# Sliding-window attention beside a state-space convolution on one core: stages put in pieces into one written order, eight shared PSUM banks, paired channels in the table product

## The chip, the cores and the metric

The kernel runs on one core of a Trainium2 chip. The metric is device time in microseconds (us) of one execution; lower is better. The engines are TensorE (PE, with PEld for its weight loads), VectorE (DVE), ScalarE (ACT), GpSimd (POOL) and SyncE (SP). SP and POOL mainly issue DMAs here. Every engine works through its own instructions in order. Matrix products land in PSUM, which has eight banks of 128 x 512 f32.

## The reference

Two independent parts are computed and joined along the last axis. S = L = 2048, D = 640, all inputs are bf16.

```python
# A: attention of 32 heads of 20 channels over the 8 positions s, s-2, ..., s-14
qkv = (x @ wqkv) -> q, k, v
logits = einsum("bhsd,bhswd->bhsw", q, kg) * 20 ** -0.5     # masked where s - 2w < 0
o = einsum("bhsw,bhswd->bhsd", softmax(logits), vg)
a = o.reshape(B, S, D) @ wo

# B: a convolution of length 2048 in each of 640 channels
K[d, l] = real(sum_n C[d, n] * exp(dt[d] * A[d, n] * l) * dt[d] * B[d, n])   # n < 192, A, B, C complex
y = irfft(rfft(u, 4096) * rfft(K, 4096))[:2048] + u * Dskip
```

## The kernel before, in words

Part B works in five chunks c of 128 channels each (four groups g of 32 channels). For a chunk it does the following.

- **Tables** (`Tables`, L314): DVE builds `Xtab` (20 powers) and `Ytab` (33 powers) from generators by complex products (`cmul`, L297: two products and two sums). `xtab` (L355) takes eight calls of `cmul`, `ypos` (L332) three, `yneg` (L347) multiplies by magnitudes that ACT made in `ymag` (L340). The generators of chunk 0 are put in place directly, those of chunks 1 to 4 go out to `Gdram` and come back by `loadx` and `loady` (L325 to L330).
- **Table product** (`kgen_part`, L386): four quarters q of eight channel indices each; every channel of a group has its own small matmul, 20 rows by 33 columns (L398 and L403), into one PSUM bank. ACT copies the bank to `Kd` (L405), and four DMAs on the POOL queue shift a part of it by one row (L383).
- **spread** (L408) and **f1** (L430), **f2** (L441): the kernel table and u are transformed to spectra. u was put into the order of `Udram` at the start: POOL loads `us`, DVE rearranges it to `uc` (L806), POOL stores it; the stage `u{c}` then loads one piece `U` (L820).
- **product** (L464) of the two spectra on DVE, after two DMAs that swap halves (L461), then **ia** (L470), the first half of the inverse. `Z` goes to DRAM for chunks 0 to 2, and stays for 3 and 4.
- **last0e, last1q** (`inverse`, L888): the second half of the inverse, with `HB`, plus u * Dskip (`uD`, L886). ACT copies to `ysb` (two buffers), SP stores it with four DMAs per piece (L902).

Part A runs in four blocks of 512 positions: `proj` (L509, PE, ACT copies `st`, SP stores to DRAM), `fetch` and `fetch_v` (L532, L541: loads of the shifted windows), `logits` (L554: ten elementwise products `prod` on DVE, sums over a head's channels on PE, exponential on ACT without a maximum, sum by PE, logarithm and exponential for the reciprocal, one product `attn` on DVE), `av` (L582: ten products `p` on DVE, sums on PE), `out_proj` (L604). `prod` and `p` share three buffers.

PSUM is shared out by tags: `a` has two banks (projections, `av`, output projection), `l` two (logits), `b` four (all of part B).

The order of the work is written out by hand: `SEQ` gives for each engine the words `stage:count`, and `chain` (L692) ties that engine's instructions together in this order. Within a stage the order is that of the code. The queues of SP and POOL are in `SEQ` too, so a DMA that waits holds everything behind it.

Of the kernel before, what the change touches and what calls it, by code (L numbers as in the profile page):

```python
# [48 lines left out]
def sel_consts_np():  # L49
# [9 lines left out]
    def add(Wm):  # L59
        full = np.zeros((128, 32), np.float32)  # L60
        for g in range(4):
            full[32 * g:32 * g + 32, 8 * g:8 * g + 8] = Wm
# [65 lines left out]
def att_consts_np():  # L128
    gs = np.zeros((128, 5, 32)); hs = np.zeros((128, 32)); sm = np.zeros((128, 128))
# [14 lines left out]
spec:15 out0:3 logits1:2 u1:8 logits1:2 out0:2 u1:2 out0:2 u1:2 out0 u1:2 logits1:4 u1:2 out0:2 spread0:8 out0:2 spread0:8 logits1:2 spread0:20
logits1:2 out0 logits1:4 spread0:8 logits1:4 out0:2 spread0:4 out0:2 spread0:2 out0 spread0:2 logits1:4 spec0:32 logits1:4 spec0 out0:4 spec0:16
out0:3 spec0:16 out0:2 spec0:15 out0 spec0:48 inv0:57 kgen20:129 inv0:7 logits1:8 kgen21 kgen22 kgen23:33 u2:2 logits1:2 kgen23:32 u2:2 logits1:2
kgen23:64 u2:2 kgen22:32 u2:2 kgen22:32 u2:4 kgen22:64 u2:4 kgen21:128 spread1:36 av1:6 spread1:8 av1:5 spread1:2 av1:8 spread1:2 av1:9 spread1:2
av1:9 spread1:2 av1:27 spec1:49 av1:15 spec1:16 av1 spec1:63 inv1:64 kgen30 kgen31:33 kgen30:32 kgen31:96 kgen30:96 kgen32 kgen33 u3:2 kgen33:32 u3:2
kgen33:32 u3:2 kgen33:32 u3:4 kgen33:32 kgen32:32 u3:6 kgen32:32 spread2:16 kgen32:32 spread2:20 kgen32:32 av1:21 spread2:8 av1:5 spread2:2 av1:8
spread2:4 av1:2 spread2:2 av1:12 spec2:6 logits2:4 spec2:26 av1:8 spec2 av1:19 spec2:16 av1:5 logits2:4 spec2:31 out1:2 logits2:4 spec2 out1:2  # L150
spec2:16 out1 spec2:15 out1:2 spec2 out1:3 spec2:15 out1:20 inv2:32 out1:7 inv2:25 kgen40:33 inv2:5 logits2:4 inv2:2 out1:2 kgen40:96 logits2:4 out1
logits2:4 kgen41 kgen42 kgen43 u4:2 kgen43:64 u4:2 kgen43:32 u4:2 kgen43:32 logits2:6 u4:2 logits2:2 u4:2 logits2:4 kgen42:32 u4:4 logits2:4 kgen42:32
u4:2 spread3:8 logits2:2 kgen42:32 spread3:8 logits2:2 spread3:12 kgen42:32 spread3:8 kgen41:32 spread3:6 kgen41:32 spread3:2 kgen41:32 spread3:6
av2:15 spread3:2 av2:33 kgen41:32 spec3:32 av2:8 spec3 av2:8 spec3:95 av2:43 inv3:32 av2:21 inv3:25 spread4:16 inv3:4 spread4:12 inv3 spread4:8 inv3:2
av2:16 spread4:16 av2:16 spec4:32 logits3:4 out2:2 spec4 logits3:2 spec4:16 logits3:2 out2:2 spec4:16 logits3:4 spec4:15 out2 spec4 logits3:4 spec4:16
out2:2 spec4:15 logits3:4 spec4 out2:2 spec4:15 logits3:4 out2:20 inv4:32 out2 logits3:4 out2:5 inv4:25 last00:18 inv4:7 logits3:12 out2:5 last01
logits3:2 last01:8 logits3:2 last01 last02 last01:8 last02:17 last03 av3:32 last03:9 last04 last03:8 av3:17 last04:17 av3:37 last05 av3:39 last05:17
av3:35 last06:10 out3:10 last06:8 out3:10 last07 out3:10 last07:17 last10:34 last11:17 out3:10 last11:17 last12:34 last13:34
""",
    mybir.EngineType.Activation: """  # L160
prep:11 am0:2 prep am0:9 weights:2 gens0:13 weights gens0:4 weights gens0:4 k0 gens0 mag0:3 k0 mag0:3 k0 mag0:2 k0 mag0:3 k0 mag0:2 q0 mag0:3 am1:11
gens1:5 q0:3 gens1 q0 v0:3 gens1 v0:2 gens1:2 k1:2 gens1 k1 gens1 k1 gens1 k1 gens1 q1 gens1 q1 gens1 q1 gens1 q1 gens1 q1 v1 gens1:2 v1 gens1 v1
gens1 v1:2 k2:2 gens1:2 k2:2 mag1:5 k2 mag1:3 q2:2 mag1:8 q2 kgen00 q2:2 kgen03 kgen02 kgen01 v2:5 k3:5 q3:5 mag2:16 kgen13 v3:2 logits0:2 v3:2 kgen10
v3 logits0:2 kgen11 kgen12 av0:2 u0:8 av0:2 spec:4 av0:2 spec:4 out0 spec:4 out0 spec:4 out0 u1:7 spread0:4 u1 out0 spread0:8 out0:2 spec0:6 out0
spec0:10 mag3:14 inv0:4 mag3:2 inv0:3 out0 kgen20 inv0 logits1:2 u2:2 logits1:2 kgen23 u2:4 kgen22 u2:2 kgen21 spread1:12 av1:2 spec1:16 mag4:8 inv1:7
mag4 inv1 mag4:7 kgen31 kgen30 u3:5 kgen33 u3:3 spread2:4 kgen32 spread2:8 av1:2 spec2:6 av1 spec2:4 av1 spec2:4 out1 spec2:2 out1:5 inv2:4 out1
inv2:4 kgen40 out1 u4:3 kgen43 u4:4 logits2:2 u4 spread3:2 logits2 spread3 logits2 spread3 kgen42 spread3:8 kgen41 spec3:16 av2:2 inv3:4 av2:2 inv3:3
spread4:4 inv3 spread4:8 av2:2 spec4:10 out2 spec4:6 out2:3 inv4:2 out2 inv4:2 out2:2 inv4:3 last00:2 inv4 logits3:2 out2 last01 logits3:2 last01
last02:2 av3:2 last03:2 av3:2 last04:2 av3:2 out3 last05:2 out3:3 last06:2 last07:2 out3:4 last10:2 last11:2 last12:2 last13:2
""",  # L170
    mybir.EngineType.DVE: """
prep:11 gens0 prep gens0:2 prep:2 gens0:2 genm0 gens0:2 genm0 gens0:2 genm0 gens0:2 genm0 gens0:2 genm0 gens0:2 genm0 gens0:2 genm0 gens0:2 genm0
gens0:2 genm0 gens0 weights genm0 ypos0 genm0 weights:10 xtab0 weights xtab0 gens1 xtab0:2 gens1 xtab0:2 gens1 xtab0:2 gens1 xtab0:2 u xtab0:8 gens1
genm1 xtab0 genm1 xtab0 gens1 xtab0:2 genm1 xtab0:4 gens1 xtab0:4 gens1 xtab0:2 gens1 ypos0 genm1 gens1:2 ypos0 gens1 genm1 gens1 ypos0 gens1 genm1
gens1 ypos0 gens1 genm1 gens1 ypos0 genm1 gens1:2 ypos0 gens1 genm1 gens1 ypos0 genm1 yneg0 gens1 yneg0 ypos0:2 genm1 ypos0:2 u yneg0:2 xtab1:22 u
xtab1:4 logits0 xtab1:4 logits0 xtab1:2 logits0 ypos1:2 logits0 ypos1:2 logits0 ypos1:2 logits0 ypos1:4 yneg1 ypos1:2 yneg1:2 u xtab2:2 yneg1 xtab2:2
logits0 xtab2:2 logits0 xtab2:2 logits0 xtab2:2 logits0 xtab2:8 logits0 xtab2 av0:8 xtab2 av0:2 xtab2 ypos2 xtab2 logits1 xtab2:4 logits1 xtab2:4
logits1 xtab2:2 logits1 ypos2 logits1 ypos2:2 logits1 ypos2:2 logits1 ypos2:2 logits1 ypos2 xtab3 ypos2 yneg2 ypos2:2 yneg2 xtab3 yneg2 prod0 xtab3
prod0:2 xtab3 prod0 xtab3:2 yneg2 xtab3:2 logits1 xtab3:2 logits1 xtab3:10 logits1 xtab3:2 av1 xtab3:4 av1 xtab3:4 av1 xtab3:2 ypos3:4 av1 ypos3:2
xtab4 ypos3:2 av1 ypos3:2 yneg3 ypos3:2 yneg3 xtab4 prod1 xtab4 prod1:2 xtab4 prod1 xtab4:2 yneg3 xtab4:2 yneg3 xtab4:2 av1 xtab4:2 av1 xtab4:2 av1  # L180
xtab4:18 av1:2 ypos4:2 logits2 ypos4:4 logits2 ypos4:2 logits2 yneg4 ypos4 yneg4 ypos4 prod2 ypos4 prod2:2 ypos4 prod2 yneg4 logits2 yneg4 logits2:7
av2:7 prod3:3 av2 prod3 av2 ud1 ud4 ud0 ud2 ud3 av2 logits3:6 prod4:3 logits3 prod4 logits3:4 av3:10
""",
# [432 lines left out]
def kernel(  # L618
# [213 lines left out]
    with at("fetch0"):  # L832
        a.fetch(0)
# [114 lines left out]
```

## Time and profile before

| | |
|---|---|
| median of three runs | 418.0 us |
| the three runs | 409.86, 418.0, 427.05 us |
| span of the profiled execution | 415.1 us (from the first to the last instruction; the page gives no other time of it) |
| PE busy | 316.8 us, 5645 matmuls |
| DVE busy | 307.1 us, 445 instructions |
| ACT busy | 262.1 us, 570 instructions |
| DMA | 70.67 MB in 78841 packets, 170 GB/s |
| table product on PE (L398 and L403) | 29.7 and 27.4 us, 1280 matmuls each |
| projections on PE (L515) | 76.4 us |
| `prod` and `p` on DVE (L562 and L592) | 48.2 and 47.4 us |
| `Xtab`, largest groups on DVE (L306 and L307) | 24.5 and 24.4 us |

How to read the profile: a line of a group gives engine, operation, output and inputs, shapes, count, busy time and the mean time of one. A line of waits gives who waited for whom, then the total in us, the number of times and the longest. "issue" is time in which an engine waited for nothing that the profile shows. In the timeline the first number is the start in us, the second the length, and the bracket is the idle time ahead of the group with what ended it. A window gives what moved in one stretch of the span.

### The profile page before, as it was taken

What the parts mean: (1) busy time and instruction counts of PE and PEld (TensorE: products, weight loads), DVE (VectorE), ACT (ScalarE), POOL (GpSimd) and SP (SyncE); (2) the same over time, 40 slices, a digit from 0 to 9 for tenths busy, and PEclk for the clock granted to TensorE, in tenths of its full rate; (3) what the DMA queues carried; (4) which work ended last, traced back from release to release, by engine and by line L of the source; (5) the groups of instructions that cost most, each with busy time, mean ns of one, the idle gap of its engine ahead of it and who ended that gap; (6) DMA issues with size and microseconds to landing.
All of it is one profiled execution on the core that took longest, in us unless ns stands there. A gap on an engine that the chain in (4) does not pass through costs nothing. (4 is left out here: it accounts for less than half of the span.)

```text
span 415.1 us, 13105 instructions
## 1 busy us (share of the span) xinstructions
PE 316.8 (76%) x5645; PEld 196.1 (47%) x5654; DVE 307.1 (74%) x445; ACT 262.1 (63%) x570; POOL 50.4 (12%) x101
## 2 busy tenths in 40 slices
PE   0569249989359988799788886799999875897781
PEld 0224114335233355356476556565666663475561
DVE  0558978995974999589999599959972765786500
ACT  0587977987004533489976596469747977573552
POOL 7453300004014010200000200011000400000000
PEclk9999959999759999589979696779999988799996
DMA  5999765668998847869308530727166499616656
GB/s 75 217 212 178 202 164 190 214 216 260 207 213 205 271 126 171 233 146 254 114 17 230 154 86 2 205 64 154 51 195 209 138 369 313 137 49 177 160 134 95
DMA packets 78841, 70.67 MB, mean 170 GB/s; under 512 B 35264, under 2 KB 73904, under 8 KB 76992
## 3 DMA queue, kind: packets, MB, share of 16 engines
q1 hardware_dynamic: 71616, 54.96, 51.3%
q0 software_dynamic: 4144, 12.18, 11.9%
q10 hardware_dynamic: 3024, 2.70, 2.9%
q8 instruction: 44, 0.72, 0.7%
q14 instruction: 13, 0.11, 0.1%
HBM read 37.82 MB, written 23.65 MB: 148 GB/s over the span
## 5 line engine op out<-in xcount | busy, mean ns | idle before, releaser
L515 PE MATMUL ps_p<-xT,w 128*128 128x512 bf16 x291 | 76.4, 409 | 20.9 <-ACT st L516 15.4
L515 PEld LDWEIGHTS <-w 128*128 128x128 bf16 x300 | 30.0, 103 | 60.3 <-issue 33.3
L562 DVE TENSOR_TENSOR prod<-qk 128x2048 bf16<-128x2048 bf16 x40 | 48.2, 1225 | 11.6 <-PE ps_l L566 8.9
L592 DVE TENSOR_TENSOR p<-vb,attn 128x2048 bf16<-128x2048 bf16 x40 | 47.4, 1224 | 12.1 <-PE ps_o L598 12.0
L438 ACT CAST A<-ps_f 128x512 bf16<-128x512 f32 x80 | 42.8, 613 | 19.0 <-PE ps_f L437 18.6
L516 ACT CAST st<-ps_p 128x512 bf16<-128x512 f32 x60 | 34.6, 586 | 23.1 <-PE ps_p L515 21.1
L456 ACT CAST Sp<-ps_f 128x512 bf16<-128x512 f32 (+1 forms) x96 | 42.4, 564 | 4.6 <-PE ps_f L452 3.5
L398 PE MATMUL ps_k<-Ytab,Xtab 128*20 128x33 bf16 x1280 | 29.7, 248 | 15.1 <-issue 15.1
L598 PE MATMUL ps_o<-p,cHs 64*32 64x256 bf16 x640 | 27.7, 297 | 12.5 <-DVE p L592 7.7
L452 PE MATMUL ps_f<-A,cT 64*128 64x128 bf16 (+1 forms) x768 | 29.4, 211 | 5.4 <-ACT Sp L456 3.5
L398 PEld LDWEIGHTS <-Xtab 128*20 128x20 bf16 x1280 | 23.3, 128 | 21.6 <-issue 20.2
L405 ACT CAST Kd<-ps_k 128x264 bf16<-128x264 f32 x20 | 7.6, 380 | 40.7 <-PE ps_k L403 40.5
L479 PE MATMUL ps_ia<-cE,Sp 128*128 128x128 bf16 x160 | 25.5, 254 | 8.0 <-DVE Sp L467 7.8
L452 PEld LDWEIGHTS <-cT 64*128 64x128 bf16 x768 | 21.7, 96 | 18.4 <-issue 17.1
L403 PE MATMUL ps_k<-Ytab,Xtab 64*20 64x33 bf16 x1280 | 27.4, 244 | 3.5 <-issue 3.5
L611 PE MATMUL ps_op<-wo,oT 128*128 128x320 bf16 x160 | 29.0, 301 | 0.7 <-ACT ob L612 0.6
L480 ACT CAST Z<-ps_ia 128x512 bf16<-128x512 f32 x40 | 22.4, 604 | 10.7 <-PE ps_ia L479 8.3
L403 PEld LDWEIGHTS <-Xtab 64*20 64x20 bf16 x1280 | 22.4, 123 | 8.0 <-issue 6.7
L479 PE MATMUL ps_ia<-cE,UT 128*128 128x128 bf16 x160 | 25.4, 253 | 0.0
L306 DVE TENSOR_TENSOR Xtab<-Xtab,Xg 128x768 bf16<-128x768 bf16 (+2 forms) x35 | 24.5, 699 | 0.3
L307 DVE TENSOR_TENSOR krtmp<-Xtab,Xg 128x768 bf16<-128x768 bf16 (+2 forms) x35 | 24.4, 698 | 0.0
L345 ACT ACTIVATE mag<-ta 128x192 bf16<-128x192 f32 x80 | 22.6, 397 | 1.2 <-DVE Ytab L351 1.2
(109 smaller groups left out, 571.0 us busy)
## 6 DMA issues: line engine op xcount, KB each, us to landing
qk<-qkd SPq DMA_DIRECT2D x20, 263.0 KB, 5.3
qkd<-st SPq DMA_DIRECT2D x8, 640.0 KB, 5.3
UT<-Sp SPq DMA_DIRECT2D x10, 512.0 KB, 6.7
Gdram<-cs SPq DMA_DIRECT2D x11, 384.0 KB, 3.0
HB<-k_HB POOLq DMA_DIRECT2D x4, 1024.0 KB, 16.1
vb<-vd SPq DMA_DIRECT2D x16, 196.5 KB, 5.0
Xg<-Gdram SPq DMA_DIRECT2D x4, 768.0 KB, 7.7
Zdram<-Z SPq DMA_DIRECT2D x3, 1024.0 KB, 8.6
```

What stands on the lines that cost most here:

```text
L398: MM(o, lhsT=X[:, :, part, col], rhs=Y[:, :, part, col], start=False, stop=False, tile_position=(0, 32 * g), skip_group_check=True)
L403: MM(o, lhsT=X[hb:hb + 64, :, part - 2, col], rhs=Y[hb:hb + 64, :, part - 2, col], start=False, stop=(part == 3), tile_position=(hb, 32 * ...
L438: nc.scalar.copy(out=A1[:].rearrange("p k r s t -> p (k r) s t")[:, :, sig, 8 * q:8 * q + 8], in_=ps[:])
L452: nc.tensor.matmul(ps[h][:, kk], lhsT=C["T"][hs, k, 64 * (1 - r):64 * (1 - r) + 128], rhs=A1[hs, k, r, s0:s1, :].rearrange("p s t -> p (s ...
L456: nc.scalar.copy(out=o, in_=ps[h][:].rearrange("p k (s t) -> p s t k", t=64))
L479: nc.tensor.matmul(ps[:, i], lhsT=X[:, h, 4 * t:4 * t + 4, :].rearrange("p g k -> p (g k)"), rhs=C["E"][:, n_, :], start=(i == 0 and n_ == ...
L515: nc.tensor.matmul(ps[:], lhsT=self.w[which][:, kt, 128 * ct:128 * ct + 128], rhs=self.xT[:, kt, 512 * sc:512 * sc + 512], start=(kt == 0) ...
L516: nc.scalar.copy(out=st[:, ct], in_=ps[:])
L562: V.tensor_tensor(out=pr[:], in0=self.qk[b][ct][:, 0, HALO:].unsqueeze(1).to_broadcast([128, 4, PB]), in1=windows(self.qk[b][ct][:, 1, 8 - ...
L592: V.tensor_tensor(out=p2[:], in0=windows(self.v[b][t][:, 2 * qp:2 * qp + 2, 0:PH], 2, 4), in1=at[:].unsqueeze(2).to_broadcast([128, 4, 2, ...
L598: nc.tensor.matmul(ps[half][32 * q:32 * q + 32, t % 2], lhsT=C["Hs"][r], rhs=p2[r, m, q2, :], start=(t % 2 == 0 and m == 0), stop=(m == 3) ...
L611: nc.tensor.matmul(ps[:], lhsT=oT[:, t, 128 * s:128 * s + 128], rhs=self.wo_sb[:, t, 320 * eh:320 * eh + 320], start=(t == 0), stop=(t == 4))
```

## The change

The stages become Python generators that stop after each piece (one PSUM tile, as a rule). A text `TRACE` names in which order the pieces are written down, and `SEQ` is replaced on every engine. What else changes:

- All PSUM tiles have one tag `ps` with eight buffers. A projection and its copies (`proj`, `spill`) are separate stages.
- The table product takes two channels in one matmul. `Xtab` gets the form [2, 20, 2, 96], and a matmul has 40 rows by 66 columns at one of two places side by side. Five parts of 7, 7, 6, 6 and 6 indices replace the four quarters, each with two zeroing matmuls. `Kd` has the form [128, 2, 33, 32], and the shift takes six DMAs a chunk. The matrices of `spread` follow the new rows.
- `cmul` writes products for the two halves. Where there is one half and at most three entries, both products are one instruction; where the entries aren't evenly spaced, each product is two. The four-entry call of `xtab` with two strides becomes two calls.
- The transposition of the parameters (`flip`) takes six matmuls per parameter and chunk instead of three.
- `us`, `uc` and `Udram` go. The stage `u{c}` loads 32 channels of each group straight from the input with four DMAs on SP (tag `Z`, one buffer, shared with `Z` and `zb`), and `f1` has four matmuls for two. `uD` is loaded straight from the input by four DMAs on the POOL queue.
- The softmax subtracts a maximum: one ACT copy, three DVE instructions and three matmuls a block. The mask is added by two matmuls in block 0, in place of seven memsets of POOL.
- `ysb` becomes `ys` with eight pieces in the place of `A1`, and its stores take turns between SP and POOL. The loads of `wqkv` go from ACT's queue to SP's, ahead of some of the loads of x.

The diff, cut to what matters:

```diff
+TRACE = """
+params params2 x0 load prep set prep x3 am0 wv weights wk wq mag0 weights mag0 gens0:2 weights gens0:6 x2 gens0:3 x1 gens0:12 k0 weights gens1 k0
...
 SEQ = {
     mybir.EngineType.PE: """
...
+prep:60 weights:120 k0:25 q0:25 v0:25 v1:16 k1:25 q1:25 v1:9 k2:25 q2:20 kgen04 kgen02:2 kgen04:2 kgen00:11 kgen03:32 kgen04 q2 kgen01:38 kgen00
...
+kgen04:4 kgen02:14 kgen01:4 kgen03 kgen00:6 kgen02 kgen03:2 kgen04 kgen01:5 kgen03:6 kgen00 kgen04:3 kgen00:26 kgen04:4 v2:10 kgen04:20 kgen02:24
+kgen00:4 logits0:8 v2:15 k3:25 logits0:8 v3:5 q3:25 v3:20 logits0:9 kgen11:18 kgen12:13 kgen10:25 kgen11:14 kgen14:38 kgen13:4 kgen11 kgen10 kgen13:15
...
     mybir.EngineType.DVE: """
...
+genm1 yneg0 genm1 ypos0:3 yneg0:3 logits0:5 xtab1:40 ypos1:7 logits0:2 yneg1 ypos1:3 yneg1:3 logits0:3 ypos2:8 yneg2
...
+ypos2:2 xtab2:8 yneg2:2 xtab2:32 yneg2 prod0:4 logits0:4 av0:10 xtab3:40 logits1:2 ypos3:3 logits1:3 ypos3:5 prod1:4 yneg3 ypos3:2 yneg3:2 logits1:2
+yneg3 logits1:7 av1:5 xtab4:12 av1 xtab4:28 av1:4 ypos4 prod2:3 ypos4:2 prod2 logits2 ypos4 logits2 ypos4:4 yneg4 ypos4 logits2:3 yneg4 ypos4 logits2
+yneg4:2 logits2:8 av2:10 logits3:6 prod3:4 logits3:7 ud0 ud3 ud1 ud2 logits3 av3:3 prod4:4 av3:7
...
     mybir.EngineType.SP: """
...
+params:7 x0:5 x3 wv wk wq x3 x2 x1:4 x3:2 weights k0 x1 q0 weights x2:3 genm1:3 v0 genm1 k1 genm1:3 x2 x3 q1 genm1 v1 genm1:3 fetch0 k2 fetch0:2 q2
+tab1 taby1:5 fetchv0 v2 fetch0:2 k3 fetchv0:5 q3 v3 tab2 fetchv0 u0:2 fftpool u0:2 taby2:5 u1:4 swap0:2 fetch1 fetchv0 tab3 inv0 taby3:5 swap1 u2:4
+swap1 fetch1:4 fetchv1:6 out0:2 tab4 fetchv1 inv1 fetch2 fetchv1 u3:4 taby4:5 swap2:2 fetchv2:6 out0:2 fetch2:2 fetchv2:2 swap3 inv2 swap3 fetch2
...
     def flip(a, diag):
-        psb = [psp.tile([128, 512], f32, name="ps_tr", tag="b", bufs=4) for _ in range(2)]
+        psb = [psp.tile([128, NCH, CW // 2], f32, name="ps_tr", tag="ps", bufs=8) for _ in range(2)]
...
-def cmul(nc, O, Y, g, t, conj, rep=None):
+def cmul(nc, O, Y, g, t, conj):
...
+    if e == 1 and merged and n <= 3:
...
+        V.tensor_tensor(out=t.rearrange("p w k r m -> p w (k r) m"), in0=kr(Y)[:, 0].unsqueeze(1).to_broadcast(sh), in1=g[:, :, 0].unsqueeze(2).to_broadcast(sh), op=A.mult)
+        for r in range(2):
+            V.tensor_tensor(out=O[:, 0, :, r], in0=t[:, 0, :, r], in1=t[:, 1, :, 1 - r], op=sub[r])
+        return
...
+    for w, o in enumerate((O, t)):
+        if merged:
+            V.tensor_tensor(out=kr(o), in0=kr(Y), in1=g[:, w].unsqueeze(2).to_broadcast([p, e, 2 * n, m]), op=A.mult)
+        else:
+            for r in range(2):
+                V.tensor_tensor(out=o[:, :, :, r], in0=Y[:, :, :, r], in1=g[:, w].unsqueeze(2).to_broadcast([p, e, n, m]), op=A.mult)
...
+    def kgen(self, q):
...
+        t0, nt = (0, 7, 14, 20, 26)[q], (7, 7, 6, 6, 6)[q]
+        ps = self.pools["psum"].tile([128, nt, NB, 2], f32, name="ps_k", tag="ps", bufs=8)
+        order = (0, 1, 2, 3) if q % 2 == 0 else (2, 3, 0, 1)
...
+        for part in order:
+            for i in range(nt):
+                for h in range(2):
+                    r = 64 * h
+                    k = slice(0, 128) if part < 2 else slice(r, r + 64)
+                    col = (32 * h if part < 2 else 64) + t0 + i
+                    MM(ps[r:r + 40, i], lhsT=X[k, :, :, part % 2, col].rearrange("p e a -> p (e a)"), rhs=Yv[k, :, part % 2, :, col], start=False, stop=(part == order[3]),
+                       tile_position=(k.start, r), skip_group_check=True)
+        nc.scalar.copy(out=Kd[:, :, :, t0:t0 + nt], in_=ps[:].rearrange("p t b e -> p e b t"))
...
-        self.nc.scalar.dma_start(out=t[:], in_=self.wqkv.rearrange("(kt k) c -> k kt c", k=128)[:, :, D * i:D * i + D])
+        self.nc.sync.dma_start(out=t[:], in_=self.wqkv.rearrange("(kt k) c -> k kt c", k=128)[:, :, D * i:D * i + D])
...
+        m1 = p.tile([128, 2, PH], bf16, name="m1", tag="rc", bufs=1)
+        nc.scalar.copy(out=m1[:], in_=ps[0][:])
+        V.tensor_tensor(out=m1[:], in0=ps[1][:], in1=m1[:], op=A.max)
+        V.tensor_tensor(out=m1[:, 0], in0=m1[:, 0], in1=m1[:, 1], op=A.max)
+        yield
+        pm = self.psp.tile([128, PH], f32, name="ps_m", tag="ps", bufs=8)
+        MM(pm[:], lhsT=C["Sw"][:], rhs=m1[:, 0], start=True, stop=True)
+        V.scalar_tensor_tensor(out=m1[:, 1], in0=m1[:, 0], scalar=-1.0, in1=pm[:], op0=A.mult, op1=A.min)
+        for mp in range(2):
+            MM(ps[mp][:], lhsT=C["ident"][:], rhs=m1[:, 1:2].to_broadcast([128, 2, PH]), start=False, stop=True, skip_group_check=True)
...
+    def u(c):
+        U = pools["fft"].tile([128, 64, 32], bf16, name="U", tag="Z")
+        for g in range(4):
+            nc.sync.dma_start(out=U[32 * g:32 * g + 32], in_=usrc[g, :, :, 32 * c:32 * c + 32])
+        yield
+        yield from f1(tc, pools, C, [U[:, :, 0:16], U[:, :, 16:32]], "BU", new_a1(c - 1), 1)
...
+            late["ys"] = pools["fft"].tile([128, 8, 1024], bf16, name="ys", tag="A1")
...
+        queue = (nc.sync, nc.gpsimd)[i % 2]
```

More of the change, by code (lines that the diff above doesn't have):

```diff
@@ L144 @@
[L144 to L147, printed above, removed]
@@ L236, in partB_prep @@
[L236 to L240 removed]
+        wk = pp.tile([128, NCH, CW // 2], f32, name="wk", tag="tmp4", bufs=4)
@@ new lines, in prod, with inv @@
+    def prod(c):
+        product(nc, late["Sp"][:, 0], late["Sp"][:, 1 + c % 2], UTs[c])
+        yield
+    def inv(c):
+        Z = pools["fft"].tile([128, 128, 32], bf16, name="Z", tag="Z") if c < 3 else late["Z34"][:, c - 3]
+        yield from ia(tc, pools, C, late["Sp"][:, 0], UTs[c][:], Z)
+        if c < 3:
+            nc.sync.dma_start(out=Zd[c][:], in_=Z[:])
+            yield
+    stage["spec"] = spec(-1)
+    for c in range(NCH):
+        stage[f"u{c}"], stage[f"spec{c}"], stage[f"swap{c}"] = u(c), spec(c), swap(c)
+        stage[f"spread{c}"], stage[f"prod{c}"], stage[f"inv{c}"] = spreading(c), prod(c), inv(c)
@@ L888, in inverse, with udq @@
+    def udq(q):
+        o = late["uD"][:, 16 * q:16 * q + 16]
+        V.tensor_tensor(out=o, in0=o, in1=small["D"][:].unsqueeze(1).to_broadcast([128, 16, 160]), op=A.mult)
+        yield
+    stage["hb"], stage["ud"] = hb(), ud()
+    for q in range(4):
+        stage[f"ud{q}"] = udq(q)
     def inverse(cs, z, l0, nl):
@@ L905, with last1 @@
+    def last1(q):
+        yield from inverse([3, 4], late["Z34"][:, :, 32 * q:32 * q + 32, :], 16 * q, 16)
     for e in range(8):
[L906 to L909 removed]
+        stage[f"last0{e}"] = last0(e)
     for q in range(4):
[L911 to L912 removed]
+        stage[f"last1{q}"] = last1(q)
@@ L913 @@
+    for word in TRACE.split():
+        name, _, n = word.partition(":")
+        for _ in range(int(n or 1)):
+            with at(None if name.endswith("pool") else name.rstrip("'")):
+                next(stage[name], None)
+    for name, pieces in stage.items():
+        with at(None):
+            assert next(pieces, "done") == "done", name
     chain()
-    fp.release()
-    att.release()
-    ip.release()
+    pools["fft"].release()
+    pools["att"].release()
+    pools["inv"].release()
```

650 lines of the change are left out of this document (341 added, 309 removed).

## The prediction

> **What bounds the kernel now.** I read the page's busy shares first, then VectorE's list of waits, then the chain that ended last with its timeline, and last two DMA windows.
>
> ```profile
> span 415.1 us, 13105 instructions
> PE 316.8 (76%) x5645; PEld 196.1 (47%) x5654; DVE 307.1 (74%) x445; ACT 262.1 (63%) x570; POOL 50.4 (12%) x101
> ...
> PEclk9999959999759999589979696779999988799996
> ```
>
> No engine is full, and PE's granted clock falls to 0.5 where it had stood idle. VectorE (DVE) and TensorE (PE) take turns. I count along DVE, because its work is one unbroken thread: it starts at 11.9 us, ends with the last `p` at 389.8, and 25.3 us of tail follow. In between it is idle for 389.8 - 11.9 - 307.1 = 70.8 us. The list of its waits names nearly all of that:
>
> ```profile
> DVE p L592 <- PE ps_o L598: 12.0, 8, 4.4
> DVE dtf L212 <- ACT dtb L210: 11.9, 1, 11.9
> DVE attn L580 <- ACT rc L579: 10.5, 3, 6.8
> DVE prod L562 <- PE ps_l L566: 8.9, 2, 6.0
> DVE UT L466 <- ACT Sp L456: 8.1, 3, 4.3
> DVE uD L886 <- DMA uD<-Udram: 5.9, 1, 5.9
> DVE Xtab L306 <- DMA Xg<-Gdram: 4.5, 1, 4.5
> DVE Ytab L306 <- DMA Ytab<-Gdram: 4.2, 2, 4.0
> ```
>
> Two more things are to be seen in PE's timeline of the table product and in the DMA window of the last 8 us:
>
> ```profile
> 106.44 1.07 PE L398 MATMUL ps_k<-Ytab,Xtab 128*20 128x33 bf16 x51
> 113.54 0.44 PE L398 MATMUL ps_k<-Ytab,Xtab 128*20 128x33 bf16 x13 [6.03 <-issue]
> 113.91 1.26 PE L403 MATMUL ps_k<-Ytab,Xtab 64*20 64x33 bf16 x64
> 115.11 1.07 PE L398 MATMUL ps_k<-Ytab,Xtab 128*20 128x33 bf16 x51
> 120.56 0.44 PE L398 MATMUL ps_k<-Ytab,Xtab 128*20 128x33 bf16 x13 [4.38 <-issue]
> ```
>
> ```profile
> DMA packets 6895, 0.86 MB, mean 108 GB/s; under 512 B 6894, under 2 KB 6894, under 8 KB 6894
> ## 3 DMA queue, kind: packets, MB, share of 16 engines
> q1 hardware_dynamic: 6894, 0.86, 72.6%
> ```
>
> The product stops every 13 + 64 + 51 = 128 matmuls (256 instructions with their weight loads) without a releaser, while the DMA engines are full. It looks like PE's instructions arriving late; the page has 18.6 us of it (15.1 + 3.5). The window prices a packet of 128 B: 0.726 x 16 x 8 us / 6895 = 13.5 ns of one engine.
>
> **The change, part by part,** as terms of start + DVE busy + DVE idle + tail = 11.9 + 307.1 + 70.8 + 25.3 = 415.1, the profiled span. The page gives no time beside the span. The three times (409.86, 418.0, 427.05) lie on both sides of it, so I add no offset: my number is both span and median.
>
> *Start, -2.4.* The weight loads leave ACT's queue, where they hold it from 4.42 to 10.33 us, before the table load (1.28) and `dtb` (0.21). The next bound is the identity: issued by 3.95, landing 5.7 later, 9.65. Start 9.5. The loads go to SP behind six transposes (38.1/20 = 1.9 us each), so `k0` begins nearer 30 than 21. That hides under PE's present stall of 13.2 us on `st` (44.5 to 57.7), and costs up to 9 us of PE without it.
>
> *DVE busy, +6.9.* Softmax maximum, per block: a 512-element maximum out of PSUM (L252, 0.69), one of 256 (between 192 at 0.26 and 384 at 0.36: 0.29), a 256-element minimum (0.42): 1.40 x 4 = 5.6. X table: the four-block product split in two adds 2x2x0.556 - 2x0.957 = 0.31 in products and 4x0.358 - 2x0.558 = 0.32 in sums; two strided products of 0.556 each become pairs of 0.355: 4 x 0.154 = 0.62. So 1.25 x 5 = 6.3. Rows of 96 instead of 192: L886, with rows of 16, takes 1.221 for 2048 elements, as L562 with rows of 512 does (1.225), so zero. Y table: 0.32 x 5 = -1.6. The four `uc` copies go: -3.3. `uD` as four of 2560 (about 1.49) for five of 1.22: -0.1. Together 314.0.
>
> *PE, about -30, counted only where DVE waits for it.* Table products go from 2560 matmuls (57 us) to 1280 with twice the columns. The pitch now is (1.28 - 0.25)/63 = 16.3 ns. Two tiles side by side with 64 columns (L452, 16 in 0.41 us) go at 14 ns; serially 66 columns would take about 29 (a full-array matmul of 128 columns goes at 56). I take 16.3, as the tiles still stand in pairs: 21 us, bounds 18 to 37. Fifty zeroing matmuls instead of 20: +0 to +5. Half the instructions halve the 18.6 us of gaps. The flips double to 180 matmuls: 0 to +12, under the 10.8 us in which PE idles from 15 to 45 us waiting for inputs, else paid there. The u transform has 32 matmuls a chunk for 16: 3.6 to 7.2 us, under ACT's eight casts (8 x 0.61 = 4.9), so at most 2.3 a chunk shows.
>
> [...]
>
> *ACT, +8:* five product casts a chunk (two of 462, three of 396 elements, near 0.55 and 0.50) for four of 0.38 are +5.4, four casts of the maximum +2.4. ACT idles 37%; uncovered it is at most 8.
>
> *DMA.* u is read five times in runs of 64 B, 8192 packets each. Between the 128 B write (13.5 ns) and the 320 B reads of `us` (40% of 16 engines x 14 us for 1.34 MB: 21.5 ns), a chunk takes 6.9 to 11.0 us of all engines; I take 9. `us`, `Udram` and `U` go (5.24 MB on the POOL queue, about 21 us, and 7 more), so the load is even. But SP now issues four DMAs of 2048 packets a chunk instead of one, and what stands behind them (`taby`, half of `swap`, `fetch`, `fetchv`) waits if the queue holds SP. U also shares one buffer with Z, so from `u2` on they wait for the landing of Z's store (8.6 us); the written order leaves a table product or an attention block in between. Price here 0; uncovered, up to 11 a chunk. [...]
>
> POOL loses 20 DMA issues for u and seven memsets, gains ten shift DMAs (0.55 each), four of `uD` and half of the output's. It idles 88%: hidden.
>
> *DVE idle, 70.8 to 50.* `ps_o` 12.0 to 6, since PE is freer and has eight shared banks instead of two. `rc` 10.5 to 17: after a block's last `prod` come 8 matmuls (0.9), ACT's cast (0.59), one matmul (0.27), two (0.5), two exponentials (1.2), four matmuls (0.4), logarithm and exponential (0.84) and eight hand-overs (0.25), 4.95 us, and in three blocks of four DVE's order has nothing in between. While PE's two added products wait for DVE, the inverse transform or table product written behind them on PE waits too, and `Z`'s casts on ACT behind that; they have a chunk's slack. `ps_l` 8.9 to 7: DVE's first five `prod` have three buffers, and on PE they stand behind all of the first table product. `Sp` 8.1 to 6. `uD` 5.9 to 0: it is loaded as soon as the tables are released. `Xg` and `Ytab` 8.7 to 3, as five `prod` now cover the first. The small waits of the opening 12.4 to 8, `qk` 2.6 to 3. Sum 50; bounds 31 (all three PE waits gone) and 71 (nothing won).
>
> *Tail, -5.* PE's work behind the last `p` stays (14.2 us). Today it waits 1.6 for `ysb` (two buffers), and one queue issues all stores. With eight buffers and two queues: 14.3 + 0.6 (last cast) + 5.4 (last cast to the end today) = 20.3.
>
> Sum: 9.5 + 314.0 + 50 + 20.3 = **393.8**, say 394.
>
> **The rivals.** *DVE leads throughout:* 31 idle, 375. For it: PE loses 30 us. Against: the softmax chain needs PE and ACT in turn. *The waits only move:* freed banks and a shorter product turn into waits for the longer softmax chain and for SP's DMAs, idle stays 71, 415: no change. For it: `rc` already costs 10.5 with a shorter chain. *Slower, SP is held by u's small packets:* if each of `u1` to `u4` holds SP for 9 us in front of transfers that DVE needs, +36, 430. For it: SP's `vb` issues took 13 us for eight while the engines were full (96.4 to 109.5). Against: POOL's transfers, which filled them, go. It decides above 32 us in all, 8 a chunk. *Nothing saved in the product:* PE at 29 ns a matmul saves 20 instead of 36; then `ps_o` stays at 12: 400, inside my case.
>
> **How the numbers follow.** My case, 382 to 409, has 0.45; DVE leading 0.22; no change 0.17; SP held 0.16. The predicted time is that of my case, 394. A measurement of this kernel can tell about 2% from no change: 409.6 and 426.4. Faster 0.67, same 0.17, slower 0.16. The range 370 to 422 leaves out the slow case and a little of the fastest.
>
> **What would show it.** DVE busy near 314 and its first instruction before 10 us; table products at about 16 ns a matmul with fewer gaps after every 128; `attn` waiting on `rc` for more than 10.5 us; no wait for `uD`; a tail near 20 us. I am wrong if DVE waits for `qk`, `vb` or `UT` behind u's loads, if PE rather than DVE has the unbroken thread, or if DVE's idle time is above 60 us.

## The result, and the profile after

The changed kernel takes 459.0 us (median of 4 runs, 457.8 to 460.0); the kernel before, run beside it, 422.5 (409.9 to 427.2). The ratio is 1.116, with a 95% interval of 1.107 to 1.124: slower by about a ninth, where I had forecast 394 us and a gain. Executions of the kernel before, and of some others, fall into a faster and a slower group (409 to 429 us in this study), and each ratio compares the faster runs of both kernels alone, so that 459.0 over 1.116 stands for 411 us before, while medians and ranges are of all runs. The profiled execution spans 456.0 us. From here on times are spans of profiled executions where terms are added up, and ratios where kernels are compared.

The page of the changed kernel, its span, busy times and granted clock:

```profile
span 456.0 us, 11011 instructions
...
PE 359.4 (79%) x4588; PEld 237.7 (52%) x4588; DVE 317.0 (70%) x482; ACT 263.8 (58%) x580; POOL 59.1 (13%) x114
...
PEclk9999998768985767978857795599998699998998
```

PE has 1057 matmuls fewer than before and is busy for 43 us more; DVE has gained 10. VectorE's list of waits, in the columns that the prediction showed (line waited for: us in total, times, longest):

```profile
DVE prod L617 <- PE ps_l L624: 49.3, 7, 19.4
DVE attn L650 <- ACT rc L649: 12.5, 4, 6.1
DVE m L638 <- PE ps_m L637: 12.1, 4, 5.6
DVE m L633 <- ACT m L632: 7.8, 2, 6.7
DVE p L662 <- PE ps_o L668: 6.5, 3, 4.5
DVE dtf L228 <- ACT dtb L226: 6.1, 1, 6.1
DVE m L633 <- PE ps_l L624: 4.8, 1, 4.8
```

One wait has grown from 8.9 to 49.3 us: `prod` for the logits' matmuls on PE. It consists mainly of two pieces of 19.4 and 18.7 us. PE's timeline around the first (start, duration, instructions) shows what stands ahead of those matmuls:

```profile
94.87 2.91 PE L439 MATMUL ps_k<-Ytab,Xtab 128*40 128x66 bf16 x43
97.71 1.46 PE L557 MATMUL ps_p<-xT,w 128*128 128x512 bf16 x3
99.10 5.36 PE L439 MATMUL ps_k<-Ytab,Xtab 128*40 128x66 bf16 x82
104.39 3.45 PE L557 MATMUL ps_p<-xT,w 128*128 128x512 bf16 x10
107.77 2.98 PE L439 MATMUL ps_k<-Ytab,Xtab 64*40 64x66 bf16 x48
110.67 0.62 PE L624 MATMUL ps_l<-prod,cGs 128*32 128x512 bf16 x8
```

L439 is the table product. 82 of its matmuls take 5.36 us: (5.36 - 0.25)/81 = 63 ns each (0.25 us is about what one takes from start to end: the mean is 248 ns in the larger group of before and 297 here, which moves the result by about 1 ns), where a matmul of half the columns went at 16.3 ns before. The logits of L624 follow at 110.67, and DVE resumes at 111.3, after 19.4 us with its three `prod` buffers full. The page's group for all of it, and the two groups of before:

```profile
L439 PE MATMUL ps_k<-Ytab,Xtab 128*40 128x66 bf16 (+1 forms) x1280 | 92.1, 297 | 0.0
```

```profile
L398 PE MATMUL ps_k<-Ytab,Xtab 128*20 128x33 bf16 x1280 | 29.7, 248 | 15.1 <-issue 15.1
L403 PE MATMUL ps_k<-Ytab,Xtab 64*20 64x33 bf16 x1280 | 27.4, 244 | 3.5 <-issue 3.5
```

Half as many matmuls take 92.1 us of PE instead of 57.1 (29.7 + 27.4). The idle column reads 0.0: the gaps after every 128 matmuls, 18.6 us before, are gone. At this pace, it seems, the instructions are there in time.

### The profile page after: what moved, and what is told of

It reads as the page before. It is cut to its first block, busy times and chain, and to the rows that moved or that the text cites. A ratio compares the mean times of both kernels' runs of the same rounds, so it can differ in the third digit from the quotient of the medians.

```text
span 456.0 us, 11011 instructions
## 1 busy us (share of the span) xinstructions
PE 359.4 (79%) x4588; PEld 237.7 (52%) x4588; DVE 317.0 (70%) x482; ACT 263.8 (58%) x580; POOL 59.1 (13%) x114
## 4 chain that ended last, share of the span: by engine, by line
PE 38%; DVE 37%; ACT 10%; issue 7%; DMA 3%; SPq 2%; DVEq 0%; ACTq 0%; POOL 0%; POOLq 0%
PE ps_k L439 19%; DVE Xtab L346 5%; DVE krtmp L341 4%; DVE Xtab L341 3%; DVE prod L617 3%; ACT A L478 3%; PE ps_ia L521 3%; DVE p L662 3%; PE ps_l L624 3%; DVE ab L312 2%; PE ps_op L686 2%; ACT Sp L497 2%; PE ps_f L476 2%; PE ps_k L431 2%; DVE cs L315 2%
## 5 line engine op out<-in xcount | busy, mean ns | idle before, releaser
L439 PE MATMUL ps_k<-Ytab,Xtab 128*40 128x66 bf16 (+1 forms) x1280 | 92.1, 297 | 0.0
L439 PEld LDWEIGHTS <-Xtab 128*40 128x40 bf16 (+1 forms) x1280 | 78.3, 151 | 18.4 <-issue 16.5
L557 PE MATMUL ps_p<-xT,w 128*128 128x512 bf16 x300 | 72.7, 400 | 17.5 <-ACT st L565 8.4
L617 DVE TENSOR_TENSOR prod<-qk 128x2048 bf16<-128x2048 bf16 x40 | 47.3, 1220 | 51.1 <-PE ps_l L624 49.3
L557 PEld LDWEIGHTS <-w 128*128 128x128 bf16 x300 | 29.9, 101 | 58.1 <-issue 22.1
L418 POOL DMA_DIRECT2D Kd<-Kd x30 | 15.2, 514 | 241.4 <-ACT Kd L441 185.3
L441 ACT CAST Kd<-ps_k 128x396 bf16<-128x396 f32 (+1 forms) x25 | 13.0, 539 | 42.6 <-PE ps_k L439 42.6
L493 PEld LDWEIGHTS <-cT 64*128 64x128 bf16 x768 | 25.3, 105 | 17.0 <-issue 15.4
L624 PE MATMUL ps_l<-prod,cGs 128*32 128x512 bf16 x160 | 22.0, 474 | 14.9 <-DVE prod L617 13.0
L346 DVE TENSOR_TENSOR Xtab<-Xtab,krtmp 128x384 bf16<-128x384 bf16 (+2 forms) x90 | 30.2, 376 | 1.4
L668 PE MATMUL ps_o<-p,cHs 64*32 64x256 bf16 x640 | 23.2, 289 | 6.9 <-DVE p L662 5.7
L686 PEld LDWEIGHTS <-oT 128*128 128x128 bf16 x160 | 14.5, 100 | 11.5 <-issue 3.8
```

Of the source, the lines that this page charges most:

```text
L346: V.tensor_tensor(out=O[:, :, :, r], in0=O[:, :, :, r], in1=t[:, :, :, 1 - r], op=sub[r])
L439: MM(ps[r:r + 40, i], lhsT=X[k, :, :, part % 2, col].rearrange("p e a -> p (e a)"), rhs=Yv[k, :, part % 2, :, col], start=False, stop=(par ...
L493: nc.tensor.matmul(ps[h][:, kk], lhsT=C["T"][hs, k, 64 * (1 - r):64 * (1 - r) + 128], rhs=A1[hs, k, r, s0:s1, :].rearrange("p s t -> p (s ...
L557: nc.tensor.matmul(ps[:], lhsT=self.w[which][:, kt, 128 * ct:128 * ct + 128], rhs=self.xT[:, kt, 512 * sc:512 * sc + 512], start=(kt == 0) ...
L617: V.tensor_tensor(out=pr[wg][:], in0=self.qk[b][ct][:, 0, HALO:].unsqueeze(1).to_broadcast([128, 4, PB]), in1=windows(self.qk[b][ct][:, 1, ...
L624: MM(ps[mp][r:r + 32], lhsT=C["Gs"][:, ct, :], rhs=pr[wg][:, 2 * mp:2 * mp + 2, PH * half:PH * half + PH], start=(ct == 0), stop=(ct == 4) ...
```

## The experiments

The theory after the result: the paired product itself is dear, for a reason that the shape of the matmul alone does not give. Rivals: the written order (it puts the logits behind the product), the granted clock (two windows of 15 us with the product in them have 0.61 and 0.73, though PE is busy throughout them), the scattered reads of the tables, and the softmax maximum as a second term (DVE's waits for `ps_m`, `m1` and one for `ps_l` make 24.7 us).

**Which form costs what (m1).** A kernel that leaves out all of the computation: only matmuls of the two table shapes and of shapes between them, 192 of each form, the tables' layout as in the kernel. "In one run" means that the columns lie side by side in memory:

```
A 20x33, tiles at 0,32,64,96    E 20x33, tiles at 0,64       I 40x66, one tile
B 40x66, tiles at 0,64          F as B, weights in one run   J 20x33, one tile
C 40x33, tiles at 0,64          G as B, moving in one run    K 20x66, four tiles
D 20x66, tiles at 0,64          H as B, both in one run      L 40x66, whole array
```

> A kernel that only loads tables and issues matmuls; it leaves out all of the computation and writes zeros, so only its TensorE rows are read. Twelve forms of the table product, 192 matmuls each, on a source line of its own, each behind 20 large matmuls that keep the array at work. Theory 'the shape is dear': 20x33 on four tiles (A) goes at 16 to 18 ns a matmul, as before the change, and 40x66 on two tiles (B) at 60 ns or more at the same granted clock. Rival 'the low clock makes it dear': B goes at 30 to 35 ns as long as the granted clock is 1.0, and doubles where it falls to 0.5. Rival 'the strided reads make it dear': B with weights and moving columns in one run (H) goes at half of B or less; F and G say which of the two reads it is. Rival 'two tiles overlap less than four': 20x33 on two tiles (E) goes at about 33 ns, twice A, and 20x66 on four (K) stays below 25.

Its PE timeline; in order forms B, F, G, H and I:

```profile
36.01 13.07 PE L47 MATMUL ps_k<-Ytab,Xtab 128*40 128x66 bf16 x192
...
96.22 11.49 PE L47 MATMUL ps_k<-Ytab,Xtab 128*40 128x66 bf16 x192
...
112.27 7.74 PE L47 MATMUL ps_k<-Ytab,Xtab 128*40 128x66 bf16 x192
...
124.55 3.26 PE L47 MATMUL ps_k<-Ytab,Xtab 128*40 128x66 bf16 x192
...
132.36 22.05 PE L47 MATMUL ps_k<-Ytab,Xtab 128*40 128x66 bf16 x192
```

By (duration - 0.25)/191: B 67 ns, F 59, G 39, H 16, I 114. The same 40x66 on the same two tiles goes at 16 ns, just what I had forecast, when both operands lie in runs, and at 67 when they are read across the tables as the kernel reads them. So it is neither the shape nor the number of matmuls. F and G show that each read alone costs: G, with only the weights scattered, 39; F, with only the moving columns scattered, 59. B is near the dearer of the two and far below their sum. One tile (I) takes 1.7 times as long as two, the whole array (L), with 114, as long as one tile, and J, 20x33 on one tile, takes 62: a scattered column costs a tile 114/66 = 1.7 to 62/33 = 1.9 ns, and tiles side by side share the time (two take 67 for the 114 of one, and 34 in E for J's 62). The kernel before had four tiles with 33 columns each (62/4 = 15.5, its 16.3); the change has two with 66 (114/2 = 57, its 63). Pairing halves the matmuls, but doubles a tile's columns and halves the tiles. C, D and E, two tiles each, took 45, 69 and 34: E, with the 33 columns of before, half of D, with 66.

The clock in windows of B, I and J (times, busy times, then the granted clock, ahead of the last two numbers):

```profile
36.00:49.00 13.00, 13.00 (x193) 12.82 (x192) 0.00 (x0) 0.56 (x1) 0.00 (x0) 1.00 0.00 1
132.40:154.40 22.00, 22.00 (x194) 21.82 (x194) 0.00 (x0) 0.51 (x1) 0.00 (x0) 0.62 0.01 1
160.90:172.90 12.00, 12.00 (x193) 11.88 (x192) 0.00 (x0) 0.57 (x1) 0.00 (x0) 1.00 0.01 1
```

B takes its 67 ns at a clock of 1.00, so the clock is not the cause. I ran at 0.62, but J at 1.00 pays no less for a column. The changed kernel shows the same: the 43 matmuls of its product from 94.87 us, at a granted clock of 0.50, take 2.91 us, (2.91 - 0.25)/42 = 63 ns each, as the 82 behind them do at 0.82. Two figures missed: A took 24 ns instead of 16 to 18, and K 44 instead of under 25. So the rate of a column from one or two tiles does not give the four tiles of A. Here two of the four tiles at a time read the same columns, where the kernel's four read four different ones; whether that is the reason was not tried.

**How far apart is far (m2).** Matmuls alone again, 40x66 on two tiles with one operand in runs and the other's columns some elements apart:

```
moving:  Yc[:, c:][:, 0:s * 65 + 1:s]    s = 1, 2, 4, 8, 16, 32, 64, 192
weights: Xc[:, c:][:, 0:s * 39 + 1:s]    s = 2, 4, 8, 16, 64, 190
```

> As m1_forms, matmuls alone (all of the computation is left out, zeros are written): seventeen forms, 192 matmuls each behind 20 large ones. The first sixteen but one are 40 weight columns by 66 moving columns on two tiles. In order: both in runs; moving columns 2, 4, 8, 16, 32, 64 and 192 elements apart (weights in runs); weight columns 2, 4, 8, 16, 64 and 190 apart (moving in runs); moving columns as 33 pairs of neighbours 384 apart; then both in runs on one tile; then 20x33, both in runs, on four tiles. Theory 'a column that does not lie beside the last costs TensorE's read more, by its distance': runs about 16 ns, the moving form rises with the distance and is near 59 at 192, the weight form near 39 at 190, and the pairs lie between, near 30. Rival 'any gap costs the full price': 2 apart is as slow as 192 apart, and only the pairs are cheaper. Rival 'runs win because the same few banks are read': the distances make no order.

Its timeline; moving columns 1, 2, 4, 8, 16 and 192 elements apart:

```profile
23.62 3.12 PE L47 MATMUL ps_k<-Ytab,Xtab 128*40 128x66 bf16 x192
33.00 3.26 PE L47 MATMUL ps_k<-Ytab,Xtab 128*40 128x66 bf16 x192
40.81 6.24 PE L47 MATMUL ps_k<-Ytab,Xtab 128*40 128x66 bf16 x192
51.59 11.95 PE L47 MATMUL ps_k<-Ytab,Xtab 128*40 128x66 bf16 x192
68.09 11.84 PE L47 MATMUL ps_k<-Ytab,Xtab 128*40 128x66 bf16 x192
...
116.87 12.29 PE L47 MATMUL ps_k<-Ytab,Xtab 128*40 128x66 bf16 x192
```

15, 16, 31, 61, 61 and 63 ns. The price of the moving columns doubles at 4 elements (8 B), doubles again at 8 (16 B), and then stays, at 58 to 63 ns, up to 384 B. Weights go from 15 (2 apart) to 20 (4) and 38 (8), and stay at 38 to 39 up to 190. Pairs of neighbours 768 B apart take 38, a little more than half the full price; 40x66 on one tile, both in runs, takes 30, and 20x33 on four tiles 8. The first theory was nearest, but the distance counts only up to 16 B; what sets that step, no run shows.

**In the kernel: the reads alone (e4).** The changed kernel, with the paired product reading runs of the same tables (so with other numbers). The last index of each piece reads as before, which keeps the order of tables and products; nothing else is changed:

```diff
+                    if part != order[3] or i < nt - 1:
+                        w, m, o = Xr[k, 2 * col:2 * col + 40], self.Y[k, 0, 1, col:col + 66], o.rearrange("p b e -> p (b e)")
```

> The changed kernel in which the paired table product reads runs: 40 neighbouring weight columns and 66 neighbouring moving columns at the end of the same tables, all but the last pair of each eighth or so, which reads as before and keeps the order of tables and products. The numbers of the table product are therefore other ones; number, shape and order of all instructions are unchanged. Theory 'the reads across the tables make the product dear': L439's 92 us become 21 to 30, DVE's wait for ps_l falls below 20, and the time comes to 394 to 415, my forecast's sum where all its other terms hold. Rival 'the matmuls are dear by their shape or the clock in this kernel': above 440. In between (415 to 440) the product was one of several wrong terms.

408.9 us (403.8 to 410.8), a ratio of 0.981 to the kernel before (0.965 to 0.997). Its page, product and longest waits:

```profile
span 408.5 us, 11010 instructions
...
PE 310.7 (76%) x4588; PEld 197.1 (48%) x4588; DVE 317.1 (78%) x482; ACT 264.0 (65%) x580; POOL 59.2 (14%) x114
...
L444 PE MATMUL ps_k<-Ytab,Xtab 128*40 128x66 bf16 (+1 forms) x1280 | 39.4, 209 | 2.6 <-DVE Ytab L391 2.4 <-issue 0.2
```

```profile
DVE prod L621 <- PE ps_l L628: 22.3, 7, 8.4
DVE attn L654 <- ACT rc L653: 10.9, 4, 4.5
...
DVE m L642 <- PE ps_m L641: 4.9, 4, 2.1
DVE m L637 <- ACT m L636: 3.6, 2, 2.5
...
DVE p L666 <- PE ps_o L672: 0.7, 2, 0.5
```

This is the decisive run. With the instructions and their order as changed and only the addresses of the reads different, 47.5 of the 456.0 us of span go, and 53 between the runs that the ratios compare (458.9 and 405.7 us on average); the sign turns. Two figures missed. The product fell by 52.7 us, to 39.4 and not to the 21 to 30 expected: a matmul takes 20 ns here ((1.83 - 0.25)/81 for a stretch of 82), and the product is cut into some 40 pieces, whose ends of about 0.25 us each make 10 us. The wait for `ps_l` fell to 22.3, not below 20.

**One channel in each matmul again (e1),** as before the change, and with it the layout of the products in `Kd`; everything else as changed:

```diff
-                for h in range(2):
-                    MM(ps[r:r + 40, i], lhsT=X[k, :, :, part % 2, col].rearrange("p e a -> p (e a)"), rhs=Yv[k, :, part % 2, :, col], ...)
+                for g in range(4):
+                    h, e = g // 2, g % 2
+                    MM(ps[32 * g:32 * g + 20, i], lhsT=X[k, e, :, part % 2, col], rhs=Yv[k, :, part % 2, e, col], ...)
```

> The changed kernel with the table product alone undone: one channel in each matmul, 2560 matmuls of 20x33 on four tiles, and with it the layout of the products in Kd; written order, banks, reads of u and softmax maximum as changed. Theory 'the paired product itself is dear': its 92 us on PE go back to about 57, the 49 us of DVE's wait prod <- PE ps_l shrink below 15, and the time falls from 459 to 405 to 425. Rival 'the written order is at fault, whatever the product costs': DVE still waits 35 us or more for ps_l, and the time stays at 445 to 459.

427.0 us, ratio 1.039 (1.028 to 1.049), 2 us above my interval. The product is back at four tiles; its group, and the wait for the logits:

```profile
L434 PE MATMUL ps_k<-Ytab,Xtab 128*20 128x33 bf16 (+1 forms) x2560 | 61.4, 249 | 2.5 <-issue 2.5
```

```profile
DVE prod L612 <- PE ps_l L619: 32.7, 7, 13.2
```

30.7 us less of product, 30.1 us less of span. But the wait for `ps_l` fell to 32.7 only, not below 15, and some 4% remain against the kernel before. So the pairing is the larger part of the loss, and not all of it.

**Pairs side by side (e9).** The moving columns read as 33 pairs of neighbours (other numbers in the product), the weights as changed:

```diff
+                        m = Yv[k, :, part % 2, 0, 2 * (col % 48):2 * (col % 48) + 2]
```

> The changed kernel in which the moving columns of the paired table product are read as 33 pairs of neighbours, 768 B apart, weights as they were: what a table with the two channels of a pair side by side would give (the numbers of the product are other ones here). m2_strides has 38.6 ns for such pairs with weights in runs, m1_forms 39 for runs with weights as they are. Theory 'the dearer of the two reads sets the pitch': 39 to 45 ns a matmul, the product near 55 to 62 us with its overhead, and on the line between e4 (39.4 us, 409) and the changed kernel (92.1 us, 459) the time is 424 to 432. Rival 'the reads add up': 55 ns or more, 440 to 450.

425.9 us, ratio 1.022 (1.015 to 1.028); the product takes 62.1 us:

```profile
L443 PE MATMUL ps_k<-Ytab,Xtab 128*40 128x66 bf16 (+1 forms) x1280 | 62.1, 250 | 0.0
```

That is within what the first theory gave: the reads don't add up in the kernel either. By this run, a table with the two channels interleaved would only bring the change back to about e1.

**The order.** The logits put ahead of other matmuls on PE, in the changed kernel (e3), with one channel a matmul (e6), and with the reads in runs (e7). In e3, from PE's written order:

```diff
-u0 logits0:5 u0:7 logits0:2 u0:24 ... spread0:15 logits0:10 u1:9
+kgen10:9 logits0:7 kgen10:16 kgen11:14 kgen14:30 logits0:10 kgen14:8 ... u0:32 ... spread0:15 u1:9
```

In e6 and e7 also:

```diff
-logits0:8 v2:15 k3:25 logits0:8 v3:5
+logits0:8 v2:15 logits0:8 k3:25 v3:5
```

> The changed kernel with PE's written order changed in one place: the last 17 matmuls of logits0 leave their places behind the second table product and stand inside it, 7 after its 40th and 10 after about its 100th matmul. Nothing else moves. Theory 'DVE starves because of the order, PE has slack': the second long wait (18.7 us at 149 to 168) goes and the time falls by 15 to 19 us, to 440 to 444. Rival 'PE has no slack here, what DVE wins it gives back at the next matmuls': 454 to 459.

> e1_unpaired with PE's written order changed in two places: the second eight matmuls of logits0 stand ahead of the 25 projections of k3 instead of behind them, and the last 17 of logits0 stand inside the second table product, as in e3_logits_ahead. Theory 'what is left of e1's loss is the order, DVE starves at 93 to 104 and at 143 to 156 us while PE has work that could wait': these two waits (11.2 and 13.2 us) lose 8 or more each, since PE idles 13.5 us for DVE between 124 and 140, and the time falls to 405 to 415. Rival 'PE has no slack': 422 to 428.

> e4_runs (the paired table product reads runs, so its numbers are other ones) with PE's written order changed in the two places of e6_unpaired_order. Theory 'with the product cheap, what is left of the wait for ps_l (22.3 us in e4 where I forecast 7) is PE's order, projections standing ahead of the logits': the time falls by 6 to 14 us from e4's 409, to 395 to 403, close to the 394 forecast. Rival 'PE has no slack even now, each projection that is put off is paid for by the tables that wait for it': 406 to 411, with another wait on DVE in the place of ps_l.

459.8, 428.8 and 407.2 us: no gain in any (ratios to the kernel before 1.119, 1.036, 0.974, each within the interval of the kernel it was made from). E3's waits show what became of the gain:

```profile
DVE prod L617 <- PE ps_l L624: 28.1, 6, 17.5
DVE krtmp L334 <- DMA Ytab<-Gdram: 17.8, 1, 17.8
```

The wait for `ps_l` falls by 21 us, and one of 17.8 appears at the next Y table: its load can't start, by the code (one Y buffer), before the delayed product has read the last one. In e6 and e7 the same wait stands at 12.7 and 8.2 us. The rival holds in all three: putting the logits ahead only changed which result DVE waits for. Other orders were not tried.

**The softmax maximum,** left out in the changed kernel (e2), with one channel a matmul (e5) and with runs (e8); the scores then go to the exponential unshifted:

```diff
-        nc.scalar.copy(out=m1[:], in_=ps[0][:])
-        V.tensor_tensor(out=m1[:], in0=ps[1][:], in1=m1[:], op=A.max)
...
-            MM(ps[mp][:], lhsT=C["ident"][:], rhs=m1[:, 1:2].to_broadcast([128, 2, PH]), ...)
```

> The changed kernel without the softmax maximum: the copy, the maximum, the minimum and the three matmuls that take it off are left out in all four blocks, so the scores are not shifted before the exponential; the rest as changed. Theory 'the maximum's chain is the second term': 5.6 us of DVE's work and most of the 12.1 + 7.8 us of waits for ps_m and m1 go, 4.8 for ps_l in the same chain too, so the time falls by 15 to 25 us, to 434 to 444. Rival 'PE with its table product sets the time and the chain lies beside it': within 5 us of 459.

> e1_unpaired (one channel a table matmul) without the softmax maximum as in e2_nomax (scores are not shifted before the exponential). Theory 'with the product out of the way the maximum's chain shows': DVE's waits for ps_m and m1 (11 us) and 5.6 us of its work go, 10 to 16 us less than e1's 427, 411 to 417, level with before. Rival 'the chain is hidden here too': 422 to 427.

> e4_runs (other numbers in the table product) without the softmax maximum, as in e2_nomax (scores not shifted). e2 and e5 lost 5 us and nothing by it, while PE was full. Theory 'the maximum was hidden by the product': here 5.3 us of DVE's work and the 11.3 us of waits for ps_m, m1 and ps_l in it come out, 395 to 403. Rival 'its wait only moves to rc, which follows from the same matmuls of PE': DVE waits over 20 us for rc and the time stays at 405 to 411.

454.3, 428.2 and 406.3 us (ratios 1.105, 1.035, 0.976): 5 us less than with it in e2, and within 1 us of it in e5 and e8 between the runs that the ratios compare, all nearest to the rival. What e2 saves in the chain comes back one step later:

```profile
DVE prod L617 <- PE ps_l L624: 48.7, 7, 19.1
DVE attn L641 <- ACT rc L640: 37.9, 4, 14.3
```

The wait for `rc` rises from 12.5 to 37.9, as the waits for `ps_m` and `m1` vanish; in e5 it is 26.3, in e8 18.9. So the theory of a second term fell: DVE would have waited for PE at the next step anyway, and the maximum only meets that wait first. It costs the changed kernel at most about 5 us.

**The kernel before, reading runs (e10),** its one-channel product unchanged otherwise (other numbers in the product):

```diff
-                        MM(o, lhsT=X[:, :, part, col], rhs=Y[:, :, part, col], ...)
+                        MM(o, lhsT=Xr[:, 2 * col:2 * col + 20], rhs=Y[:, 0, 1, col:col + 33], ...)
```

> The kernel before with its table product (one channel a matmul, 20x33 on four tiles) reading runs at the end of its tables, the last of each quarter as before (the product's numbers are other ones). m2_strides has 8.1 ns for the form in runs where the kernel has 16.3. Theory 'the scattered reads set the pace before the change as well': the product's 57 us on PE fall to 33 or less, the instruction gaps of 18.6 us stay or grow, and the time falls by 5 to 20 us, to 396 to 412. Rival 'instructions arrive no faster than that, so nothing is won': the gaps take all of it, 412 to 418.

417.6 us, ratio 1.007 (0.999 to 1.015). The two groups of its product:

```profile
L406 PE MATMUL ps_k<-Ytab,Xtab 64*20 64x33 bf16 x1280 | 17.8, 184 | 5.1 <-issue 5.0
L399 PE MATMUL ps_k<-Ytab,Xtab 128*20 128x33 bf16 x1280 | 17.2, 184 | 28.6 <-issue 25.8 <-DVE Ytab L353 2.8
```

The product fell from 57.1 to 35.0 us, and the gaps without a releaser rose from 18.6 to 30.8. Together they make 65.8 us for 2560 matmuls, 26 ns each. The gaps take over half (12.2) of the 22.1 us that the reads save, and the rest doesn't show in the time. The rival is nearer.

## Why the prediction was wrong

The sum was start 9.5 + DVE busy 314.0 + DVE idle 50 + tail 20.3 = 393.8. DVE's first instruction, its busy time, and the end of its last `p` in each trace give:

| | start | DVE busy | DVE idle | tail | span |
|---|---|---|---|---|---|
| before | 11.9 | 307.1 | 70.8 | 25.3 | 415.1 |
| forecast | 9.5 | 314.0 | 50 | 20.3 | 393.8 |
| after | 6.1 | 317.0 | 109.2 | 23.7 | 456.0 |
| e4, reads in runs | 6.2 | 317.1 | 61.9 | 23.3 | 408.5 |
| e1, one channel | 6.2 | 318.5 | 77.0 | 24.2 | 425.9 |

**The step that failed** is in the paragraph on PE: "I take 16.3, as the tiles still stand in pairs: 21 us, bounds 18 to 37." Measured were 63 ns and 92.1 us, far outside both bounds. I took 16.3 ns for the price of a matmul. By m1 it is better read as four tiles at about 65 ns each, side by side (J, one such tile alone, took 62, though A, four of them, took 24 and not 16). With half the tiles and twice the columns in each, the same rate per column makes four times 16.3, 65 ns, and 63 came. The trace of before held the warning: by the row that I used (L452, 14 ns, two tiles of half the rows, columns in runs) a tile reads 64 columns in 28 ns, 0.44 ns each (m2 later gave 30 for 66 on one tile), while the table product needed 65 ns for 33, 2 ns each. I set the two pitches side by side, took their likeness for confirmation, and did not ask why one read cost 4.5 times the other. The bound of 29 ns came from columns in runs as well, so both ends lacked the scattered read. Two lines that I showed held a second warning: 51 table matmuls take 1.07 us at 106.44 and again at 115.11, where the granted clock is 1.00 and 0.50, so it was not the array's pace that set theirs.

By the two profiled spans, 47.5 of the miss of 62.2 us are the reads (after against e4), and 53 of 65 by the runs that the ratios compare. More than half come through `ps_l` (49.3 after, 22.3 in e4, forecast as 7): I had named the mechanism ("on PE they stand behind all of the first table product") and priced it with the wrong product. Another 17 come through `ps_m`, `ps_o` and `m1`, which wait for PE or for its results too.

**What remains** is e4's 408.5 against 393.8. DVE idle is 11.9 above the 50: `ps_l` with 22.3 + 2.8 for 7 is 18 us above, and the softmax chain (`rc`, `ps_m`, `m1`) with 19.4 for 17 another 2.4. `ps_o`, `Sp` and the tables' waits came out 10 us lower than forecast together, the opening and `qk` 2 lower, and nearly 4 are small waits that the forecast did not count. That DVE waits longer for the logits than before, though the product is shorter, goes with its earlier start: it ends its first table at 87 us instead of 98, while PE runs without a pause until 118 in e4. E7's order doesn't cure it. What would stays open. In the same way e1's remaining 4% against the kernel before is not one wait: DVE has 11.4 us more work and 6 more idle, against 5.7 of start.

**Point by point.** The start came 3.4 us sooner than forecast, DVE busy within 3.0, the tail 3.4 longer. `uD`'s wait went, as forecast. The rival of the slower side, SP held by u's packets, did not occur: DVE waits 2.2 us for `Ytab`'s loads and 1.6 for `qk`, and PE's wait for u is small, one line in the changed kernel's list for PE:

```profile
PE ps_f L476 <- DMA U<-in_B_u_dram: 2.8, 2, 2.0
```

So the sign that I gave a chance of 0.16 came by a path that no rival had. The rival "nothing saved in the product", 29 ns and 400 us, had the right place with half the price. That the product's gaps are instructions arriving late is borne out by e10, where they grow as the matmuls get shorter, though no row shows it directly; there was nothing of them to save with the product at 63 ns.

None of the kernels that compute everything beats the kernel before. E4, e7 and e8 are about 2% faster, but their product reads other columns than the result needs. Tables whose product reads lie in runs would have to be written column by column; what DVE would pay for that was not tried.

## What to carry to other kernels

Before merging small matmuls, multiply their pitch by the number of tiles that run side by side: here the price belonged to a tile, and to a column that it read (m1: 62 ns for 33 scattered columns on one tile, 114 for 66). Compare that price per column with another matmul of the same trace; if it is several times higher (here 2 ns against 0.44), suspect the operand's layout, and try the form in a kernel of matmuls alone before making matmuls wider on fewer tiles. When DVE's waits add up to a large sum behind one engine, don't take a line of its list for a gain: e2 and e3 each removed waits of over 20 us, and the time fell by 5 us at most.

## What the runs showed of the hardware that I had not expected

- Moving columns 16 to 384 B apart cost TensorE four times what columns in runs do (m2: 58 to 63 against 15 ns for 66 on two tiles), columns 8 B apart twice as much as runs (31), columns 4 B apart hardly more (16).
- Scattered weights cost about as much per column as scattered moving columns (m2: 38 ns for 40 columns, 61 for 66), and the two reads overlap: 67 for both, 39 and 59 for either alone (m1).
- The granted clock fell to 0.61 in a window of the changed kernel's product in which PE was busy all the time, and to 0.62 with one tile of 40x66 in m1, but stayed at 1.00 there with two tiles and the same reads. What decides it is open; the scattered matmuls kept their 63 ns at 0.50 and at 0.82. The window of the changed kernel:

```profile
90.00:105.00 15.00, 15.00 (x187) 11.29 (x184) 1.23 (x1) 0.58 (x1) 0.00 (x0) 0.61 0.33 85
```
